# Zero products between periods, smaller GpSimd pieces and 136 score blocks on VectorE in a gated sum of two attentions

## The chip, the cores and the metric

The kernel runs on one core of a Trainium2 chip. A core has TensorE (PE; its weight loads are listed apart as PEld), VectorE (DVE), ScalarE (ACT), GpSimd (POOL), and SyncE (SP), which issues the transfers. The metric is the device time of one execution in microseconds (us); lower is better. A profiled execution also gives the span from the first instruction of the program to the last, the busy time of each engine and TensorE's granted clock.

## The reference, cut to what matters

```python
x = A_x                                            # 1 x 2048 x 512, bf16
g = sigmoid((x * gate_w).sum(-1, keepdims=True))
# A: full attention, 32 heads of 16
p = softmax(einsum("bhqd,bhkd->bhqk", q, k) * 16 ** -0.5)
a = einsum("bhqk,bhkd->bhqd", p, v) -> (S, 512) @ A_wo
# B: each query sees 8 keys, at distances 0, 2, ..., 14
logits = einsum("bhsd,bhswd->bhsw", q, k[pos - 2 * w]) * 16 ** -0.5   # masked below 0
b = einsum("bhsw,bhswd->bhsd", softmax(logits), v[pos - 2 * w]) -> (S, 512) @ B_wo
return g * a + (1 - g) * b
```

## The kernel before

**Attention A.** Queries come in 4 chunks of 512, heads in 8 groups of 4. A *period* is one chunk and one head group; there are 32, ordered so that two chunks alternate over the 8 groups and then the other two. A period has 16 key tiles x 4 heads = 64 score *blocks* of 128 keys x 512 queries. Most blocks go to ScalarE: TensorE writes the scores of a set of three blocks, then of a set of two, into the banks `ring` (`qk`, line 942), ScalarE takes the exponential of the whole set into `pT` (`ex`, 948), and TensorE multiplies with V into the accumulator `acc` (`pv`, 961; `pv_mm`, 909). There is one `acc` bank for all periods. After the last product of a period VectorE copies it out, transposed, into `accT` (`po1`, 1058), and the next period can start to write it; then come a reciprocal (`rden`), a scaling (`ott`) and a second transpose (`oat`).

Some blocks of each period, `n_dve` (line 20), go to VectorE instead: 3 in each of the first 18 periods, then 5, then 6, 129 in all. They come in groups of up to three (`d_group`, 980; groups are made in 1040). TensorE writes each block's scores into a bank `misc` (`dq`), VectorE evicts it into `dt` (`p1`), and three polynomial steps of 128 x (512 times the group's blocks) make the exponential (`p2` and `p3` write `dg`, `p4` writes `pd`); TensorE then adds their product into `acc` as well (`dpv`). There are two `misc` banks. All projections, transposes and the sums of B use them in turn (`misc_ps`).

**Attention B** goes in 16 tiles of 128 queries (`b_tile`, 682). GpSimd multiplies q with eight shifted copies of k, 512 columns an instruction (`prods`, 752), TensorE sums over a head's 16 columns (`sums`), the softmax is on VectorE, ScalarE (one exponential of 128 x 256, `lg`) and GpSimd, and GpSimd multiplies with the shifted v (`avs`, 846) and adds up (`ava`, 860). TensorE transposes the result (`fin`, 880) for the output projection.

**Order.** All instructions of an engine stand in one order that a planner makes before the program is built (`list_schedule`, 98). It holds an estimated duration for each operation (`PE`, `PORT`, `TMUL`, lines 80 to 88) and a due time, and it plays the engines forward, taking the operation that is due first among those that can start. `PORT` is what a VectorE operation takes longer while GpSimd is busy; `TMUL` is the cost of a GpSimd product. Banks and buffers are tokens with a capacity (`Res`, `Tok`).

**Zero products.** The planner also keeps an account of how much TensorE has done over the last 3.4 us (`covered`, 130). Where TensorE would idle over 0.3 us and the account is under 8.6 passes, it books extra products, `o.pre` (line 184). They are products of zeros with ones that are added into the accumulator:

```python
    def zeros(pi, n, first=()):
        js = [j for j in list(first) + list(range(4)) if 1 <= todo[(pi, j)] < NT]
        for k in range(n if js else 0):
            mm(acc_tiles[pi][32 * j:32 * j + 32, :], z32[:], ones_t[:], False, False, tile_position=(0, 32 * j))
```

So they are issued only while a head's accumulation is open; between two periods `js` is empty and nothing is issued, though the account holds them. `warm` (439) issues products of the same kind into a `misc` bank; the old kernel uses it eight times before the first set.

In the profile most lines carry the number of the recording helper (L272 for VectorE, ScalarE, GpSimd and SyncE, L281 for TensorE), so instructions are told apart by their tiles.

Of the kernel before, what the change touches and what calls it, by code (L numbers as in the profile page):

```python
# [9 lines left out]
ALU = mybir.AluOpType  # L10
# [6 lines left out]
CFG = dict(  # L17
    set_sizes=(3, 2),
    chunks_at_once=2,
    n_dve=(3,) * 18 + (5,) * 9 + (6,) * 5,  # L20
    dve_tiles=2,
    b_start=26.0,
    b_space=46.7,
# [3 lines left out]
H = 32  # L27
# [29 lines left out]
class Op:  # L57

    def __init__(self, eng, occ, fn, dl, deps=(), alloc=(), use=(), lat=None, rel=0.0, name="",
                 dense=0, fill=False, after=(), cls="a"):  # L60
        self.sw, self.row = 0.0, False
        if isinstance(occ, str):
            self.row = occ in ("qk", "dq")
            occ, self.sw, lat, dense = PE[occ]
        self.eng, self.occ, self.fn, self.dl, self.rel, self.name = eng, occ, fn, dl, rel, name
        self.dense, self.fill, self.filled = dense, fill, 0
        self.after = [d for d in after if d is not None]
        self.deps, self.alloc = [d for d in deps if d is not None], list(alloc)
        self.lat = (occ if not callable(occ) else occ(False)) + LAT[eng] if lat is None else lat
        self.done = self.ex = None  # L70
        self.cls, self.clock, self.pre = cls, False, 0
        self.slack = SLACK if eng == "pe" else (0.0, 0.0)
        for tk in list(alloc) + list(use):
            tk.ops.append(self)
# [9 lines left out]
          vk=(0.50, 0.05, 0.68, 2), sums=(0.46, 0.15, 0.78, 2), turn=(0.37, 0.02, 0.53, 1), fin=(0.23, 0.10, 0.54, 1),  # L84
          zc=(0.84, 0.10, 0.98, 4), ztr=(0.11, 0.0, 0.24, 0), tr0=(1.0, 0.0, 1.2, 0), tr=(0.55, 0.0, 0.78, 0),
          warm7=(3.2, 0.0, 3.4, 0), warm1=(0.45, 0.0, 0.6, 0))
PORT = dict(p2=0.50, p3=0.75, p4=0.75, ab=0.35, po2=0.48, selk=0.25)
TMUL = 1.35
SLACK, DSLACK = (0.2, 0.2), 2.0
AHEAD = dict(pe=0.10, dve=0.12, act=0.25, pool=0.5, sp=0.0)  # L90


# [2 lines left out]
    return lambda busy: us + (PORT[key] if busy else 0.0)  # L95


def list_schedule(ops):

    INF = 1e18  # L100
    free = {e: 0.0 for e in LAT}
# [24 lines left out]

    out, cover = [], []
    psw = 0.0

    def covered(t):  # L130
        return sum(w * (min(b, t) - max(a, t - SPAN)) for a, b, w in cover if b > t - SPAN and a < t) / PASS
# [10 lines left out]
    def due(o):  # L142
        return o.dl + lag[o.cls]

    def window():
# [8 lines left out]
        end = p.t + p.occ if p.done is not None else max(free["act"], getattr(p, "ready", 0.0)) + p.occ  # L154
        return t, max(t, end - QK_LEAD)

    while len(out) < len(ops):
        best = None
        for e, cs in cand.items():
            if not cs:  # L160
                continue
            es = [(max(free[e], avail(o)), o) for o in cs]
            w = window() if e == "pe" else None
            if w:
                es = [(max(t, w[0]) if o.ex is None and t + o.occ + max(o.sw, 0.0) > w[1] and t < due(o) + LATE else t, o) for t, o in es]
            t0 = min(x[0] for x in es)
            if t0 < INF and (best is None or t0 < best[0]):
                best = (t0, e, es)
# [11 lines left out]
        if e == "pe":  # L180
            idle = t - free[e]
            act = covered(t)
            if t > 30.0 and idle > GAP_MIN and act < ACTIVE:
                o.pre = min(int((idle - 0.05) / FILL), int(ACTIVE - act + 1))
                add_cover(free[e], free[e] + o.pre * FILL, 1.0)
                act = covered(t)
            n = o.dense
            if o.fill and act + n < ACTIVE:
                for k in (2, 1):
                    more = k * FILL  # L190
                    if act + n + k - 1 < ACTIVE and (w is None or t + occ + o.sw + more <= w[1] or act + n + k - 1 < ACTIVE_LOW):
                        o.filled = k
                        occ, lat, n = occ + more, lat + more, n + k
                        break
            add_cover(t, t + (PASS * n if not o.row else PASS), 0.75 if o.row else 1.0)
            psw = o.sw
        o.t, o.done = t, t + max(occ, lat)
        free[e] = t + occ
        if o.ex is not None:
            nq += 1  # L200
        if o.clock:
            lag[o.cls] = t - o.clock
        cand[e].remove(o)
# [10 lines left out]
def kernel(  # L214
# [457 lines left out]
    def opb(*a, **k):  # L672
        return op(*a, cls="b", **k)
# [8 lines left out]
    def b_tile(t):  # L682
# [69 lines left out]
        def prods(hf, w0, w1):  # L752
            def s():
                if w0 == 0:
                    st["prod", hf] = work.tile([128, WH, DC, 128], FP32, name="prod", tag="prod", bufs=2)
                for w_ in range(w0, w1):
                    b0 = PAD - DIL * (hf * WH + w_)
                    G.tensor_tensor(out=st["prod", hf][:, w_], in0=kT_tiles[t][:, :, b0:b0 + 128], in1=st["qT"][:], op=ALU.mult)
            return s

        def sums(hf, w0, w1):
# [84 lines left out]
        def avs(hf, w0, w1):  # L846
            def s():
                if hf + w0 == 0:
                    st["ob"] = work.tile([128, D], FP32, name="ob", tag="ob", bufs=1)
                if w0 == 0:  # L850
                    st["av", hf] = work.tile([128, WH, D], FP32, name="prod", tag="prod", bufs=2)
                vsh, attn, pr_ = st["vsh"], st["lg"], st["av", hf]
                for w_ in range(w0, w1):
                    a0 = attn[:, :, hf * WH + w_:hf * WH + w_ + 1]
                    G.tensor_tensor(out=pr_[:, w_, :].rearrange("p (h d) -> p h d", d=DH),
                                    in0=vsh[:, hf * WH + w_, :].rearrange("p (h d) -> p h d", d=DH),
                                    in1=_ap(a0, [list(a0.ap[0]), [W, H], [0, DH]]), op=ALU.mult)
            return s

        def ava(hf):  # L860
            def s():
                pr_ = st["av", hf]
                for w_ in range(2):
                    G.tensor_tensor(out=pr_[:, w_, :], in0=pr_[:, w_, :], in1=pr_[:, 2 + w_, :], op=ALU.add)
                G.tensor_tensor(out=(pr_[:, 0, :] if hf else st["ob"][:]), in0=pr_[:, 0, :], in1=pr_[:, 1, :], op=ALU.add)
                if hf:
                    st["obb"] = work.tile([128, D], BF16, name="obb", tag="obb", bufs=1)
                    G.tensor_tensor(out=st["obb"][:], in0=st["ob"][:], in1=pr_[:, 0, :], op=ALU.add)
            return s
        for hf in range(2):  # L870
            tpv = tok("prod", 2)
            for w0 in (0, 2):
                a = opb("pool", 2 * TMUL - 0.2, avs(hf, w0, w0 + 2), tb + 22 + 10 * hf + 1.5 * w0, deps=[a, lv],
                        alloc=([tpv] if w0 == 0 else []) + ([tob] if hf + w0 == 0 else []), use=[tlg, tvs] + ([tpv] if w0 else []))
            a = opb("pool", 4.9 + 1.6 * hf, ava(hf), tb + 28 + 10 * hf, deps=[a], alloc=[tbb] if hf else [], use=[tpv, tob])
        tk = tok("misc", 2)
        if cb not in obt_tok:
            obt_tok[cb] = tok("obt", 2)
# [11 lines left out]
        def oe():  # L890
            V.tensor_copy(out=obt_tiles[cb][:, :, tl * 128:(tl + 1) * 128], in_=st["ptp"][:])
        a = opb("pe", "fin", fin, tb + 50, deps=[a] + o_obt[-1:], alloc=[tk] + ([obt_tok[cb]] if tl == 0 else []), use=[tbb] + ([obt_tok[cb]] if tl else []))
        o_obt.append(opb("dve", 0.34, oe, tb + 51, deps=[a], use=[tk, obt_tok[cb]]))

    for t in range(NT):
# [36 lines left out]
    for k, us in enumerate(sets):  # L932
# [25 lines left out]
        for pi in pis:  # L958
            mine = [(s_, t, j) for s_, (p_, t, j) in enumerate(us) if p_ == pi]

            def pv(pi=pi, mine=mine, st=st):
                zeros(pi, st["op", pi].filled, [j for _, t, j in mine])
                for s_, t, j in mine:
# [2 lines left out]
            o = op("pe", "pv", pv, tn - 2.0, fill=not first, deps=[b] + [o_v[(4 * periods[pi][1] + j, t)] for _, t, j in mine]  # L966
                   + ([] if first else [o_first[pi]]),
                   alloc=[acc_tok[pi]] if first else [], use=[tp] + ([] if first else [acc_tok[pi]]), name=f"pv{k}")
            o.slack = (0.0, 0.0)
            st["op", pi] = o  # L970
            if first:
                o_first[pi] = o
# [2 lines left out]
                t_first[pi] += sum(1 for _, t, j in mine if t == 0)  # L975
                o_t0[pi] = o

    d_last = [None, None]

    def d_group(pi, gr, lo, hi):  # L980
        c_, i = periods[pi]
# [38 lines left out]
                pv_mm(pi, t, j, st["pd"][:, q_, :], vd_all[:, t - (NT - NTD)])  # L1020

        dur = 0.14 + 0.54 * n
        prev2, prev = d_last
        for q_, (t, j) in enumerate(gr):
            tx = tok("misc", 2)
            a = op("pe", "dq", dq(q_), hi - 7.5 + q_, deps=[o_q[pi], o_kc[i][t // TPC], prev2] + ([o_k0[t // TPC]] if i == 0 else []), alloc=[tx], use=[q_tok[pi]],
                   rel=lo, name=f"dq{pi}")
            prev2, prev = prev, op("dve", 0.67, p1(q_), hi - 6.5 + q_, deps=[a], alloc=[td] if q_ == 0 else [],
                                   use=[tx] + ([td] if q_ else []), after=[prev])
        d_last[:] = prev2, prev  # L1030
        a = op("dve", shared(dur, "p2"), p2, hi - 4.2, deps=[prev], alloc=[tg], use=[td])
        a = op("dve", shared(dur, "p3"), p3, hi - 2.6, deps=[a], use=[tg, td])
        a = op("dve", shared(dur, "p4"), p4, hi - 1.0, deps=[a], alloc=[tp], use=[tg, td])
        a = op("pe", "dpv", pv, hi, deps=[a, o_t0[pi]] + [o_v[(4 * i + j, t)] for t, j in gr],
               use=[tp, acc_tok[pi]], name=f"dpv{pi}")
        a.slack = (DSLACK, 0.0)
        o_pv[pi].append(a)

    for pi in range(NP):
# [143 lines left out]
        b = op("dve", 0.67, t_ev, E2 + 1 + tt, deps=[b, a], alloc=[tos], use=[tk, tfb])  # L1183
        op("sp", 0.6, dout, E2 + 2 + tt, deps=[b], use=[tos], lat=2.2)

    order = list_schedule(ops)
    if cfg.get("debug"):
        cfg["debug"](order)
    for o in order:
        if o.pre and acc_tiles:  # L1190
            zeros(max(acc_tiles), o.pre)
        o.fn()


# [28 lines left out]
```

## Time and profile before

| | us |
|---|---|
| median of 3 runs (lowest to highest) | 923.12 (919.32 to 923.97) |
| the profiled execution | 919.24 |
| its span | 917.5 |
| ScalarE busy | 885.3 |
| TensorE busy | 828.3 |
| VectorE busy | 647.1 |
| GpSimd busy | 554.3 |

The page gives each engine's busy time and its share of the span. In a group of instructions the columns are: output and inputs, shape, count, busy time in us, mean ns of one, and the idle time of the engine just before them with what ended most of it. In a timeline the columns are start, length in us, engine and operation; instructions that follow each other closely are merged into one row (x44 is 44 of them, and the shape shown is that of the first), and the idle time before a row stands in brackets with what ended it. The table by stretches gives, for each, the busy time and count of each engine, the granted clock, and the share and rate of transfers. A granted clock of 1.00 is full speed; a clock of 0.73 over 25 us is the mean of full and half speed.

### The profile page before, as it was taken

Reading aid. Unit: us, or ns where it says so; the run is one execution under the profiler, and the core shown is the slowest. Engines: PE = TensorE matmul, PEld = TensorE weight load, DVE = VectorE, ACT = ScalarE, POOL = GpSimd, SP = SyncE. Lnnn points to the kernel's source line nnn. Section 1 sums busy time; section 2 is a strip of 40 time slices with the busy share of each in tenths; the row PEclk is TensorE's granted clock in tenths of the full one; section 3 lists DMA queues with packets and bytes.
Section 4 is the critical chain, followed back from the end, with each engine's and each line's share of the span. In section 5 each row is a group of like instructions: output and inputs, shape, how many; then the busy total and the mean of one; then the engine's idle time right before and its main releaser. Section 6 shows DMA issues by size and latency. Waiting matters only on the chain.

```text
span 917.5 us, 20157 instructions
## 1 busy us (share of the span) xinstructions
PE 828.3 (90%) x8520; PEld 306.6 (33%) x8520; DVE 647.1 (71%) x815; ACT 885.3 (96%) x794; POOL 554.3 (60%) x412
## 2 busy tenths in 40 slices
PE   7999989999999999998999999989898889899886
PEld 4333333333433333333333232333332333222222
DVE  4596676776567765676934677787868686978874
ACT  4999999999999999999999999999999999989996
POOL 1347492687567696677574839985979883910000
PEclk9999999999999999999999998999998999979999
DMA  8101010010101010101010100110010110000001
GB/s 272 57 4 51 2 43 12 7 47 7 47 8 53 1 48 7 47 7 53 1 64 30 53 8 1 52 47 8 1 53 2 47 52 2 1 1 1 1 1 46
DMA packets 27330, 28.58 MB, mean 31 GB/s; under 512 B 1604, under 2 KB 26724, under 8 KB 27240
## 3 DMA queue, kind: packets, MB, share of 16 engines
q1 hardware_dynamic: 27240, 27.30, 9.2%
q8 instruction: 66, 1.08, 0.5%
q14 instruction: 24, 0.20, 0.1%
HBM read 23.08 MB, written 4.22 MB: 30 GB/s over the span
## 4 chain that ended last, share of the span: by engine, by line
ACT 56%; issue 20%; PE 18%; DVE 5%; DMA 1%; SPq 0%; DVEq 0%; ACTq 0%
ACT pT L272 55%; PE acc L281 6%; PE ring L281 6%; PE misc_ps L281 4%; DVE dg L272 2%; PE misc L281 1%; DVE pd L272 1%; DMA xld<-in_A_x_dram 1%; ACT lg L272 1%; DVE dt L272 0%; DVE osb L272 0%; ACT xT L272 0%; DVE accT L272 0%; DVE qt L272 0%; DVE kmax_all L272 0%
## 5 line engine op out<-in xcount | busy, mean ns | idle before, releaser
L272 ACT ACTIVATE pT<-ring 128x1536 bf16<-128x1536 f32 (+2 forms) x768 | 874.7, 1353 | 12.1 <-PE ring L281 11.3
L281 PE MATMUL ring<-qt,kt_all 32*128 32x512 bf16 x1919 | 311.0, 387 | 71.1 <-ACT pT L272 66.3
L281 PE MATMUL acc<-pT,vp_all 128*17 128x512 bf16 (+1 forms) x1919 | 298.6, 390 | 1.1 <-DVE accT L272 0.9
L272 POOL TENSOR_TENSOR prod<-kTb,qTb 128x512 f32<-128x512 bf16 x128 | 167.8, 1334 | 99.1 <-DVE qTb L272 87.0
L281 PEld LDWEIGHTS <-kt_all 32*128 32x128 bf16 x2048 | 109.6, 91 | 342.7 <-issue 329.5
L272 POOL TENSOR_TENSOR prod<-vsh,lg 128x512 f32<-128x512 bf16 x128 | 181.4, 1441 | 3.1 <-PE misc_ps L281 1.9
L272 POOL TENSOR_TENSOR prod<-prod 128x512 f32<-128x512 f32 x80 | 130.3, 1645 | 1.3
L272 DVE TENSOR_SCALAR dt<-misc 128x512 f32<-128x512 f32 x129 | 87.1, 683 | 58.6 <-PE misc L281 53.4
L281 PEld LDWEIGHTS <-vp_all 128*17 128x17 bf16 (+1 forms) x1919 | 68.6, 88 | 160.9 <-issue 156.9
L281 PE MATMUL misc_ps<-xT,wst 128*32 128x512 bf16 x1024 | 100.2, 383 | 1.1 <-ACT kt_all L272 0.8
L281 PE MATMUL acc<-ones_t,z 128*32 128x512 bf16 x271 | 94.7, 397 | 0.0
L272 DVE SCALAR_TENSOR_TENSOR pd<-dg,dt 128x1536 uint16<-128x1536 bf16 (+1 forms) x46 | 94.1, 2046 | 0.3
L272 DVE SCALAR_TENSOR_TENSOR dg<-dt,dg 128x1536 bf16<-128x1536 uint16 (+1 forms) x46 | 93.0, 2022 | 0.4
L272 DVE SCALAR_TENSOR_TENSOR dg<-dt 128x1536 bf16<-128x1536 uint16 (+1 forms) x46 | 90.5, 1966 | 1.2
L272 POOL TENSOR_TENSOR lg<-lg,rr 128x256 f32<-128x256 f32 x16 | 10.1, 628 | 134.3 <-DVE rr L272 47.5
L281 PE MATMUL misc<-qt,kt_all 32*128 32x512 bf16 x129 | 47.9, 390 | 2.7 <-DVE qt L272 1.6
L281 PE MATMUL misc_ps<-prod,hsel 128*32 128x128 f32 x1024 | 43.0, 276 | 1.5 <-DVE dt L272 0.8
L272 DVE TENSOR_SCALAR qt<-misc_ps,rowc 128x512 bf16<-128x512 f32 x32 | 25.7, 803 | 20.4 <-PE misc_ps L281 20.3
L281 PE MATMUL misc_ps<-xT,bw 128*128 128x128 bf16 x512 | 39.2, 220 | 0.0
L272 DVE TENSOR_TENSOR qt<-qt,misc_ps 128x512 bf16<-128x512 bf16 x32 | 21.7, 678 | 17.6 <-PE misc_ps L281 17.6
L281 PEld LDWEIGHTS <-bw 128*128 128x128 bf16 x512 | 28.7, 98 | 15.9 <-issue 15.4
L281 PEld LDWEIGHTS <-wst 128*32 128x32 bf16 x1024 | 27.8, 95 | 18.6 <-issue 5.5
(85 smaller groups left out, 620.6 us busy)
## 6 DMA issues: line engine op xcount, KB each, us to landing
vsh<-v_scr SPq DMA_DIRECT2D x16, 1024.0 KB, 5.5
xld<-in_A_x_dram SPq DMA_DIRECT2D x4, 512.0 KB, 7.4
v_scr<-vs SPq DMA_DIRECT2D x16, 128.0 KB, 1.7
out_dram<-osb SPq DMA_DIRECT2D x16, 128.0 KB, 1.7
wst<-in_A_wqkv_dram SPq DMA_DIRECT2D x3, 512.0 KB, 7.0
bw<-in_B_wqkv_dram SPq DMA_DIRECT2D x1, 1536.0 KB
bwo<-in_B_wo_dram SPq DMA_DIRECT2D x1, 512.0 KB, 13.4
woarr<-in_A_wo_dram SPq DMA_DIRECT2D x8, 64.0 KB, 10.0
```

The costliest lines, as they stand in the source:

```text
L272: return chain_on(key, f(*a, **k))
L281: return chain(nc.tensor.matmul(out, lhsT=lhsT, rhs=rhs, start=start, stop=stop, **kw))
```

## The change

- `n_dve`: periods 1 to 14 take 3 and 4 blocks in turn; 136 blocks in all, and ScalarE has 1912 instead of 1919. Four blocks make two groups of two.
- GpSimd's products and sums are issued in pieces of 256 columns, so 368 more instructions.
- Planner costs: `PORT` is lowered, `TMUL` and the cost of the sums are raised.
- Planner rules: near the end of a period (at most two of its products into `acc` left) a long polynomial step (`long`) that would run into the copy of `acc` is planned behind it (`turn`). The score products of a VectorE group do not start before the last polynomial step of the group ahead (`behind`). The transposes of a B tile are planned 4 us after GpSimd's end.
- Zero products are booked for `acc` only while a period's accumulation is partly done; between periods they go into a free `misc` bank (`pre_misc`, through `warm`), if there is time after the bank's last reader, and they take the bank's turn.

```diff
-    n_dve=(3,) * 18 + (5,) * 9 + (6,) * 5,
+    n_dve=(3, 4) * 7 + (3,) * 4 + (5,) * 9 + (6,) * 5,
...
-PORT = dict(p2=0.50, p3=0.75, p4=0.75, ab=0.35, po2=0.48, selk=0.25)
-TMUL = 1.35
-SLACK, DSLACK = (0.2, 0.2), 2.0
+PORT = dict(p2=0.30, p3=0.42, p4=0.42, ab=0.20, po2=0.28, selk=0.15)
+TMUL = 1.58
+SLACK, DSLACK, TURN = (0.2, 0.2), 2.0, 0.5
...
+    def turn():
+
+        p = min((p for p in acc_all if acc_left[p] > 0), default=None)
+        if p is None or acc_left[p] > 2:
+            return None
+        rest = [o for o in acc_ops[p] if o.done is None]
+        if any(d.done is None for o in rest for d in o.deps):
+            return None
+        return max(max(d.done + o.slack[0] for d in o.deps) for o in rest) + TURN
...
+            if e == "dve":
+                tt = turn()
+                if tt is not None:
+                    es = [(max(t, tt) if o.long and t + o.occ(False) > tt and t < tt else t, o) for t, o in es]
...
-                o.pre = min(int((idle - 0.05) / FILL), int(ACTIVE - act + 1))
-                add_cover(free[e], free[e] + o.pre * FILL, 1.0)
+                k = min(int((idle - 0.05) / FILL), int(ACTIVE - act + 1))
+                if any(0 < acc_left[p] < acc_all[p] for p in acc_all):
+                    o.pre = k
+                    add_cover(free[e], free[e] + k * FILL, 1.0)
+                elif not any(tk.res is misc for tk in o.alloc):
+                    n = len(misc.order)
+                    us = [u.done for u in misc.order[n - misc.cap].ops] if n >= misc.cap else [0.0]
+                    if None not in us:
+                        b = max([free[e]] + us)
+                        k = min(k, int((t - b - 0.05) / FILL))
+                        if k > 0:
+                            o.pre_misc = k
+                            add_cover(b, b + k * FILL, 1.0)
...
-                    G.tensor_tensor(out=st["prod", hf][:, w_], in0=kT_tiles[t][:, :, b0:b0 + 128], in1=st["qT"][:], op=ALU.mult)
+                    for c in range(0, DC, 2):
+                        G.tensor_tensor(out=st["prod", hf][:, w_, c:c + 2], in0=kT_tiles[t][:, c:c + 2, b0:b0 + 128],
+                                        in1=st["qT"][:, c:c + 2], op=ALU.mult)
...
+                for d0 in range(0, D, D // 2):
+                    ds = slice(d0, d0 + D // 2)
+                    for w_ in range(2):
+                        G.tensor_tensor(out=pr_[:, w_, ds], in0=pr_[:, w_, ds], in1=pr_[:, 2 + w_, ds], op=ALU.add)
...
+        a.slack = (4.0, 0.2)
...
-        prev2, prev = d_last
+        prev2, prev, behind = d_last
...
-                   rel=lo, name=f"dq{pi}")
+                   rel=lo, after=[behind], name=f"dq{pi}")
...
         a = op("dve", shared(dur, "p2"), p2, hi - 4.2, deps=[prev], alloc=[tg], use=[td])
+        a.long = True
...
+        if o.pre_misc:
+            warm(o.pre_misc)()
         o.fn()
```

More of the change, by code (lines that the diff above doesn't have):

```diff
@@ L70, in __init__ @@
         self.done = self.ex = None
-        self.cls, self.clock, self.pre = cls, False, 0
+        self.cls, self.clock, self.pre, self.pre_misc, self.acc, self.long = cls, False, 0, 0, None, False
         self.slack = SLACK if eng == "pe" else (0.0, 0.0)
@@ L95, in shared, with list_schedule @@
     return lambda busy: us + (PORT[key] if busy else 0.0)
-def list_schedule(ops):
+def list_schedule(ops, misc):
     INF = 1e18
@@ L128, in list_schedule @@
     psw = 0.0
+    acc_left, acc_all, acc_ops = {}, {}, {}
+    for o in ops:
+        if o.acc is not None:
+            acc_all[o.acc] = acc_left[o.acc] = acc_all.get(o.acc, 0) + 1
+            acc_ops.setdefault(o.acc, []).append(o)
     def covered(t):
@@ L183, in list_schedule @@
             if t > 30.0 and idle > GAP_MIN and act < ACTIVE:
-                o.pre = min(int((idle - 0.05) / FILL), int(ACTIVE - act + 1))
-                add_cover(free[e], free[e] + o.pre * FILL, 1.0)
+                k = min(int((idle - 0.05) / FILL), int(ACTIVE - act + 1))
[11 more added lines that the diff above has]
+                            add_cover(b, b + k * FILL, 1.0)
+                            f = Op("pe", 0.0, None, 0.0)
+                            f.done = b + k * FILL + 0.25
+                            tk = Tok(misc)
+                            tk.ops.append(f)
+                            misc.order.append(tk)
                 act = covered(t)
@@ L200, in list_schedule @@
             nq += 1
+        if o.acc is not None:
+            acc_left[o.acc] -= 1
         if o.clock:
@@ L853, in s @@
                 for w_ in range(w0, w1):
[L854 to L857, printed above, removed]
+                    for h0 in range(0, H, H // 2):
+                        a0 = attn[:, h0:h0 + H // 2, hf * WH + w_:hf * WH + w_ + 1]
+                        ds = slice(h0 * DH, (h0 + H // 2) * DH)
+                        G.tensor_tensor(out=pr_[:, w_, ds].rearrange("p (h d) -> p h d", d=DH),
+                                        in0=vsh[:, hf * WH + w_, ds].rearrange("p (h d) -> p h d", d=DH),
+                                        in1=_ap(a0, [list(a0.ap[0]), [W, H // 2], [0, DH]]), op=ALU.mult)
             return s
@@ L862, in s @@
                 pr_ = st["av", hf]
-                for w_ in range(2):
-                    G.tensor_tensor(out=pr_[:, w_, :], in0=pr_[:, w_, :], in1=pr_[:, 2 + w_, :], op=ALU.add)
-                G.tensor_tensor(out=(pr_[:, 0, :] if hf else st["ob"][:]), in0=pr_[:, 0, :], in1=pr_[:, 1, :], op=ALU.add)
                 if hf:
                     st["obb"] = work.tile([128, D], BF16, name="obb", tag="obb", bufs=1)
-                    G.tensor_tensor(out=st["obb"][:], in0=st["ob"][:], in1=pr_[:, 0, :], op=ALU.add)
+                for d0 in range(0, D, D // 2):
+                    ds = slice(d0, d0 + D // 2)
+                    for w_ in range(2):
+                        G.tensor_tensor(out=pr_[:, w_, ds], in0=pr_[:, w_, ds], in1=pr_[:, 2 + w_, ds], op=ALU.add)
+                    G.tensor_tensor(out=(pr_[:, 0, ds] if hf else st["ob"][:, ds]), in0=pr_[:, 0, ds], in1=pr_[:, 1, ds], op=ALU.add)
+                    if hf:
+                        G.tensor_tensor(out=st["obb"][:, ds], in0=st["ob"][:, ds], in1=pr_[:, 0, ds], op=ALU.add)
             return s
@@ L872, in b_tile @@
             for w0 in (0, 2):
-                a = opb("pool", 2 * TMUL - 0.2, avs(hf, w0, w0 + 2), tb + 22 + 10 * hf + 1.5 * w0, deps=[a, lv],
+                a = opb("pool", 2 * TMUL, avs(hf, w0, w0 + 2), tb + 22 + 10 * hf + 1.5 * w0, deps=[a, lv],
                         alloc=([tpv] if w0 == 0 else []) + ([tob] if hf + w0 == 0 else []), use=[tlg, tvs] + ([tpv] if w0 else []))
-            a = opb("pool", 4.9 + 1.6 * hf, ava(hf), tb + 28 + 10 * hf, deps=[a], alloc=[tbb] if hf else [], use=[tpv, tob])
+            a = opb("pool", 5.7 + 2.3 * hf, ava(hf), tb + 28 + 10 * hf, deps=[a], alloc=[tbb] if hf else [], use=[tpv, tob])
         tk = tok("misc", 2)
@@ L968 @@
                    alloc=[acc_tok[pi]] if first else [], use=[tp] + ([] if first else [acc_tok[pi]]), name=f"pv{k}")
-            o.slack = (0.0, 0.0)
+            o.slack, o.acc = (0.0, 0.0), pi
             st["op", pi] = o
@@ L976 @@
                 o_t0[pi] = o
-    d_last = [None, None]
+    d_last = [None, None, None]
     def d_group(pi, gr, lo, hi):
@@ L1026, in d_group @@
             a = op("pe", "dq", dq(q_), hi - 7.5 + q_, deps=[o_q[pi], o_kc[i][t // TPC], prev2] + ([o_k0[t // TPC]] if i == 0 else []), alloc=[tx], use=[q_tok[pi]],
-                   rel=lo, name=f"dq{pi}")
+                   rel=lo, after=[behind], name=f"dq{pi}")
             prev2, prev = prev, op("dve", 0.67, p1(q_), hi - 6.5 + q_, deps=[a], alloc=[td] if q_ == 0 else [],
                                    use=[tx] + ([td] if q_ else []), after=[prev])
-        d_last[:] = prev2, prev
         a = op("dve", shared(dur, "p2"), p2, hi - 4.2, deps=[prev], alloc=[tg], use=[td])
+        a.long = True
         a = op("dve", shared(dur, "p3"), p3, hi - 2.6, deps=[a], use=[tg, td])
+        a.long = True
         a = op("dve", shared(dur, "p4"), p4, hi - 1.0, deps=[a], alloc=[tp], use=[tg, td])
+        a.long = True
+        d_last[:] = prev2, prev, a
         a = op("pe", "dpv", pv, hi, deps=[a, o_t0[pi]] + [o_v[(4 * i + j, t)] for t, j in gr],
                use=[tp, acc_tok[pi]], name=f"dpv{pi}")
-        a.slack = (DSLACK, 0.0)
+        a.slack, a.acc = (DSLACK, 0.0), pi
         o_pv[pi].append(a)
@@ L1184 @@
         op("sp", 0.6, dout, E2 + 2 + tt, deps=[b], use=[tos], lat=2.2)
-    order = list_schedule(ops)
+    order = list_schedule(ops, res["misc"])
     if cfg.get("debug"):
```

## The prediction

> **What bounds the kernel now.** I read the page's busy shares and the slices first, then ScalarE's timeline, then the stretches with their granted clock.
>
> ```profile
> PE 828.3 (90%) x8520; PEld 306.6 (33%) x8520; DVE 647.1 (71%) x815; ACT 885.3 (96%) x794; POOL 554.3 (60%) x412
> PEclk9999999999999999999999998999998999979999
> ```
>
> ScalarE is busy 96% and its only large work is the 767 exponentials of the score sets. The clock row shows that TensorE's granted clock fell in a few slices. What ScalarE lost is not its idle time (12.1 us in its group): successive exponentials overlap by 0.1 to 0.4 us, so a late set first eats the overlap. I therefore measure pace, start to start, on its timeline.
>
> ```profile
> 255.89 49.82 ACT L272 ACTIVATE pT<-ring 128x1536 bf16<-128x1536 f32 x44
> 305.51 0.51 ACT L272 ACTIVATE lg<-lg 128x256 f32<-128x256 f32 x1
> ...
> 799.20 9.25 ACT L272 ACTIVATE pT<-ring 128x1536 bf16<-128x1536 f32 x8 [0.51 <-PE ring L281]
> 809.36 2.37 ACT L272 ACTIVATE pT<-ring 128x1536 bf16<-128x1536 f32 x2 [0.91 <-PE ring L281]
> 812.37 2.36 ACT L272 ACTIVATE pT<-ring 128x1536 bf16<-128x1536 f32 x2 [0.64 <-PE ring L281]
> 815.37 1.45 ACT L272 ACTIVATE pT<-ring 128x1536 bf16<-128x1536 f32 x1 [0.64 <-PE ring L281]
> 817.28 91.17 ACT L272 ACTIVATE pT<-ring 128x1024 bf16<-128x1024 f32 x81 [0.46 <-PE ring L281]
> ```
>
> Sets alternate between three blocks and two, so 44 sets are 110 blocks, and from 255.89 to 305.51 they took 49.62 us: 0.4511 us a block with nothing in the way. The exponentials run from 21.23 to 908.45 (817.28 + 91.17), 887.2 us. At that pace 1919 blocks are 865.7; the 16 softmax exponentials of B, one slot of 0.30 us each (305.51 to the next start at 305.81), are 4.8. **Lost: 16.7 us.** Where: from 799.20 to 817.28 there are 13 sets, 33 blocks, 14.9 us at pace, but 18.1 passed: 3.2 lost. The same sum over the other stretches whose granted clock is below 1.00 gives 1.2 (305.81 to 337.68), 2.05 (539.64 to 562.89), 0.8 (634.95 to 668.23) and 2.07 (683.33 to 699.84). Together 9.3 us go with five falls of the clock; 7.4 are spread elsewhere, largest 1.25 near 757.
>
> ```profile
> 795.00:820.00 25.00, 22.48 (x136) 5.01 (x135) 19.24 (x19) 21.77 (x20) 11.18 (x6) 0.73 0.01 1
> 820.00:908.50 88.50, 78.63 (x720) 25.07 (x720) 61.04 (x68) 88.45 (x79) 0.00 (x0) 1.00 0.01 4
> ```
>
> The columns are TensorE, weight load, VectorE, ScalarE, GpSimd, granted clock. A fall begins at the end of a period. This is the one at 802:
>
> ```profile
> 800.71 1.76 DVE L272 SCALAR_TENSOR_TENSOR dg<-dt 128x1536 bf16<-128x1536 uint16 x1
> ...
> 802.39 0.71 DVE L272 STREAM_TRANSPOSE accT<-acc 128x512 f32<-128x512 f32 x1
> 802.96 0.39 PE L281 MATMUL ring<-qt,kt_all 32*128 32x512 bf16 x3 [0.95 <-ACT pT L272]
> ```
>
> A long polynomial step holds VectorE, the copy of acc waits behind it, and TensorE, which has no accumulator to write, stands idle 0.95 us; matmuls take 0.61 us in place of 0.39 from 804.20 on.
>
> **The change, part by part.** *136 blocks on VectorE.* Seven blocks leave ScalarE: 7 x 0.4511 = **-3.2 us** on the path. On VectorE they are 14 groups of two in place of 7 of three, and seven more evictions of 0.683.
>
> ```profile
> L272 DVE SCALAR_TENSOR_TENSOR dg<-dt 128x1536 bf16<-128x1536 uint16 x37 | 76.9, 2079 | 1.1
> ...
> L272 DVE SCALAR_TENSOR_TENSOR dg<-dt 128x1536 bf16<-128x1536 uint16 x6 | 10.5, 1758 | 0.2
> ```
>
> The first row is the whole run, the second the stretch 826 to 908, where GpSimd has ended. A three-step polynomial of three blocks costs 2079 + 2112 + 2108 = 6.30 us beside GpSimd and 1758 + 1732 + 1738 = 5.23 without. For two blocks the run has 1505 + 1650 + 1790 = 4.95, or by proportion 3.49 alone. So VectorE gets 14 x 3.49 - 7 x 5.23 + 4.8 = +17 at the least and 14 x 4.95 - 7 x 6.30 + 4.8 = +30 at the most. It hides under VectorE's 270 us idle; without that cover it would come back as late products of VectorE's blocks at a period's end.
>
> *GpSimd in pieces of 256.* The order of the built program has 368 more GpSimd instructions.
>
> ```profile
> 788.30 1.27 POOL L272 TENSOR_TENSOR ob<-prod 128x512 f32<-128x512 f32 x1
> ...
> L272 POOL TENSOR_TENSOR lg<-lg,rr 128x256 f32<-128x256 f32 x16 | 10.1, 628 | 134.3 <-DVE rr L272 47.5 <-ACT pT L272 37.7 <-PE misc L281 16.1
> ```
>
> An undisturbed 512-column step takes 1.27 and a 256-column one 0.628, so two pieces cost 1.26: nothing. The upper bound, a fixed 0.1 us for each added piece, is 37 us over the 16 tiles of B. GpSimd's last instruction ends at 806.33 (803.67 + 2.66), and in the changed order its last tile is folded in after block 1775 of 1912 instead of 1733 of 1919, some 20 us later; the end of the run is 100 us away, which covers even the bound. What it brings: a long VectorE step that meets GpSimd waits for the instruction in flight. The excess is 1.07 a group of three (37 groups: 39.6), 1.46 a group of two (nine: 13.1), and 0.37 at each ott step (786 in the run, 413 alone; 32: 11.9): 64.6 us, of which half goes if the instruction in flight is half as long, 32. That pays for the added blocks, and the steps in front of the copy of acc get shorter. For GpSimd I take no gain: a product stands at 2.62 (789.52) instead of 1.09 when VectorE's step came first, and the steps are as long as before.
>
> *Copies kept free, later scores.* Long polynomial steps are held back when the copy of acc is due. VectorE then idles up to one step (1.76) a period, 56 us in 32 periods at the most, within its 270; behind the held step stand the rest of its group and then that group's product into acc, for which only the next copy waits, most of a period (27 us) later. The late copy at 802 cost 0.95 us of TensorE. Score products for VectorE stand behind the preceding group's last step in the plan, so they no longer hold a misc bank early; what they delay is VectorE's eviction (dt), which already waits 53.4 us for them in VectorE's own idle time. The first transposes of a finished B tile are planned 4 us after GpSimd instead of 0.2; they are needed only by the output projections of their chunk, a wait that costs nothing until then. The smaller port costs and larger GpSimd cost only shift the plan.
>
> *Zero products between periods.* Today's plan books products between periods that are never issued (with no open accumulator the list is empty) and counts them as cover. The changed program issues 26 into a misc bank, at 14 places, all but one after block 1510; products into acc go from 271 to 257. A zero product takes 0.397 as a row and 0.21 in step; it fills an idle TensorE, so it costs nothing while its bank is free.
>
> *Sum.* Of the 9.3 lost with the clock, 3.2 lie in the late third where the new products are; the other four places (6.1) get none and profit only from the quicker copy and from a plan that no longer counts absent work: I take 0.6 of it, 3.7, so 6.9 in all, with bounds 0 and 9.3. Of the 7.4 spread losses I take 0.65, 4.8, since the largest two I could follow (1.25 near 757, 0.65 before 799.20) stand behind VectorE: the chain of waits runs through dg, dg and pd from 747.69 to 755, and at 798.08 TensorE waits 0.89 for qt; bounds -2 (new waits) and 7.4. The head (21.23) and tail (9.05) stay. 919.24 (the profiled execution: span 917.5 and 1.7 around it) - 3.2 - 6.9 - 4.8 = **904 us**. The runs' median, 923.12, is 3.9 above that execution; I put it down to more falls of the clock in those runs, which the change would thin too, and keep 904.
>
> **The rivals.** *The clock falls as often.* For: four of five places get no product, and five falls at 31 boundaries leave much to chance. Against: the phantom cover is gone everywhere. Time: 919.2 - 3.2 - 2.4 (half of my spread gain) = 913.6. "TensorE: Matmul & The Clock Gate", section Part 1, in the Trainium skill gives this rival its mechanism: activity is judged in free-running windows of 3.4 us, so the phase of a run decides. The granted stretches here (0.73 of 25 us is 13.6 us at half clock, four such windows) agree.
>
> *It does not do what it says.* The plan's new costs may fit the chip no better, and waits only move: the seven blocks alone give 916.0.
>
> *Slower: the zero products block TensorE.* They stand in order before the next scores and need a bank that VectorE has read. Behind a polynomial step (2.1) with one set in ScalarE's hand (0.9) each place loses 1.2; at all 14 places 16.8, so 919.2 - 3.2 + 16.8 = 932.8. It decides from eight places on (9.6 us, which beats 3.2 and the 4.6 of the bound below). Against: the plan puts them only where the bank is free with time over, and the waits of TensorE's misc products for VectorE and ScalarE sum to 10.4 us in the whole run, none over 1.5.
>
> **How the numbers follow.** A measurement of this kernel tells 0.5%, 4.6 us, from no change. Forecast 0.68, clock falls on 0.16, blocks alone 0.08, blocked TensorE 0.08. Faster: all of the first, 0.10 of the second, 0.01 of the third: 0.79; same 0.13; slower 0.08. Range: the low end is 919.2 - 3.2 - 9.3 - 7.4 = 899.3, less 3 for a pace between the 0.4511 used and the fastest pairs; the high end takes in the clock rival and stops short of the third: 896 to 915.
>
> **What would show it.** Right: ScalarE at 0.451 a block from first to last set, at most two stretches with a clock below 1.00, long steps near 1.9 rather than 2.08, GpSimd's pieces near 0.55 to 0.63 where nothing blocks them. Wrong: half-clock stretches at the same four boundaries, ScalarE waiting for ring right behind zero products, or GpSimd running past 880 and the last projections behind it.

## The result, and the profile after

The changed kernel takes 906.72 us (median of 4 runs, 904.43 to 907.0); the kernel before 921.39 (4 runs, 919.32 to 923.97). The ratio is 0.986, with a 95% interval of 0.982 to 0.990, so faster by 1.4%; the medians lie 14.7 us apart. The profiled execution took 906.7, its span is 904.6 (before: 919.24 and 917.5). Of the runs further down, one execution of e8 took 3622.6 us and is left out of every number.

From the page, busy times and granted clock:

```profile
PE 822.2 (91%) x8532; PEld 308.6 (34%) x8532; DVE 638.5 (71%) x843; ACT 879.4 (97%) x791; POOL 637.1 (70%) x780
PEclk9999999999999999999999999999999999999999
```

No slice shows a granted clock below nine tenths any more. VectorE has 53 groups of polynomial steps instead of 46 and is busy 9 us less; GpSimd is busy 83 us more.

ScalarE's timeline, a clean stretch and the places where a set came late:

```profile
340.74 54.37 ACT L309 ACTIVATE pT<-ring 128x1024 bf16<-128x1024 f32 x48
394.79 0.61 ACT L309 ACTIVATE lg<-lg 128x256 f32<-128x256 f32 x1
...
551.66 18.33 ACT L309 ACTIVATE pT<-ring 128x1536 bf16<-128x1536 f32 x16
570.48 12.75 ACT L309 ACTIVATE pT<-ring 128x1536 bf16<-128x1536 f32 x11 [0.48 <-PE ring L318]
...
772.14 32.82 ACT L309 ACTIVATE pT<-ring 128x1024 bf16<-128x1024 f32 x29
805.29 54.49 ACT L309 ACTIVATE pT<-ring 128x1536 bf16<-128x1536 f32 x48 [0.34 <-PE ring L318]
860.25 34.99 ACT L309 ACTIVATE pT<-ring 128x1536 bf16<-128x1536 f32 x31 [0.46 <-PE ring L318]
```

The pace is unchanged: 48 sets, 120 blocks, in 54.05 us from 340.74 to 394.79, 0.4504 a block. The exponentials run from 21.54 to 895.24 (860.25 + 34.99), 873.7 us. At 0.4511 the 1912 blocks are 862.5 and B's exponentials 4.8, so 6.4 us are lost, where 16.7 were before. The stretches with a lowered clock:

```profile
551.66:583.00 31.34, 29.04 (x290) 10.81 (x290) 25.45 (x31) 30.86 (x29) 30.71 (x36) 0.95 0.02 6
772.14:805.29 33.15, 29.32 (x229) 9.55 (x228) 26.89 (x30) 32.82 (x30) 32.60 (x34) 0.96 0.02 8
805.29:895.24 89.95, 81.00 (x727) 25.31 (x724) 56.23 (x60) 89.47 (x79) 4.47 (x3) 0.98 0.01 4
```

Against the pace they lost 0.67 (68 blocks), 0.67 (72) and 1.09 (197): 2.4 us, where five stretches lost 9.3 before. Narrower stretches show each of the three falls:

```profile
564.00:574.00 10.00, 9.49 (x68) 2.33 (x66) 8.43 (x7) 9.52 (x9) 10.00 (x10) 0.83 0.04 13
799.00:809.00 10.00, 9.02 (x57) 2.26 (x52) 8.03 (x6) 9.66 (x10) 9.69 (x10) 0.83 0.01 2
854.00:864.00 10.00, 8.87 (x55) 2.46 (x55) 8.06 (x7) 9.54 (x10) 0.00 (x0) 0.83 0.00 0
```

10 us at 0.83 are 3.4 us at half clock; the fall before at 802 lasted 13.6. They also stand elsewhere. In the kernel before, each of the five falls begins 1.0 to 3.1 us behind a copy of `acc` (copies at 330.8, 554.3, 663.2, 691.3 and 802.4, falls at 334, 556, 665, 692 and 805). In the changed kernel they begin in the middle of a period, at 567, 803 and 857, 11 us or more behind the last copy. So in this execution the falls at the ends of periods are gone, and the three that are left stand in mid-period.

VectorE's steps and GpSimd's pieces, mean ns behind the busy time:

```profile
L309 POOL TENSOR_TENSOR prod<-kTb,qTb 128x256 f32<-128x256 bf16 x256 | 209.5, 849 | 106.9 <-DVE qTb L309 89.7 <-PE misc_ps L318 16.8
...
L309 DVE SCALAR_TENSOR_TENSOR dg<-dt 128x1536 bf16<-128x1536 uint16 x30 | 58.6, 1952 | 1.0
...
L309 DVE SCALAR_TENSOR_TENSOR dg<-dt 128x1024 bf16<-128x1024 uint16 x23 | 31.1, 1351 | 0.7
```

A three-block step costs 1952 ns instead of 2079 (1758 without GpSimd), so VectorE waits less for GpSimd. A pair of pieces costs GpSimd 2 x 849 = 1.70 us in place of 1.334: undisturbed, one takes 0.607 at the least, and a whole one took 1.039, and each piece may have to wait for a VectorE step (not followed one by one). GpSimd ends at 809.9 all the same (806.3 before).

### The profile page after: what moved, and what is told of

The parts are those of the page before. It is cut to its first block, busy times and chain, and to the rows that moved or that the text cites. A ratio compares the mean times of both kernels' runs of the same rounds, so it can differ in the third digit from the quotient of the medians.

```text
span 904.6 us, 20592 instructions
## 1 busy us (share of the span) xinstructions
PE 822.2 (91%) x8532; PEld 308.6 (34%) x8532; DVE 638.5 (71%) x843; ACT 879.4 (97%) x791; POOL 637.1 (70%) x780
## 4 chain that ended last, share of the span: by engine, by line
ACT 62%; issue 21%; PE 15%; DVE 1%; DMA 1%; ACTq 0%; SPq 0%; DVEq 0%
ACT pT L309 61%; PE ring L318 5%; PE acc L318 5%; PE misc_ps L318 4%; ACT lg L309 1%; DMA xld<-in_A_x_dram 1%; PE misc L318 1%; ACT xT L309 0%; DVE osb L309 0%; DVE kmax_all L309 0%; PE pxt L495 0%; PE misc_ps L820 0%; PE misc_ps L930 0%; ACT kt_all L309 0%; ACTq L1268 0%
## 5 line engine op out<-in xcount | busy, mean ns | idle before, releaser
L309 ACT ACTIVATE pT<-ring 128x1536 bf16<-128x1536 f32 x765 | 870.1, 1387 | 4.5 <-PE ring L318 4.3
L318 PE MATMUL ring<-qt,kt_all 32*128 32x512 bf16 x1912 | 302.5, 383 | 69.5 <-ACT pT L309 63.9
L318 PE MATMUL acc<-pT,vp_all 128*17 128x512 bf16 (+1 forms) x1912 | 289.0, 385 | 1.1 <-DVE accT L309 0.9
L309 POOL TENSOR_TENSOR prod<-kTb,qTb 128x256 f32<-128x256 bf16 x256 | 209.5, 849 | 106.9 <-DVE qTb L309 89.7
L318 PEld LDWEIGHTS <-kt_all 32*128 32x128 bf16 x2048 | 112.4, 91 | 339.2 <-issue 325.6
L309 POOL TENSOR_TENSOR prod<-vsh,lg 128x256 f32<-128x256 bf16 x256 | 207.0, 840 | 7.7 <-PE misc_ps L318 7.0
L309 POOL TENSOR_TENSOR prod<-prod 128x256 f32<-128x256 f32 x160 | 140.4, 893 | 2.5
L309 DVE TENSOR_SCALAR dt<-misc 128x512 f32<-128x512 f32 x136 | 91.7, 686 | 68.7 <-PE misc L318 65.7
L318 PE MATMUL misc_ps<-xT,wst 128*32 128x512 bf16 x1024 | 97.5, 384 | 0.8 <-ACT kt_all L309 0.8
L318 PE MATMUL acc<-ones_t,z 128*32 128x512 bf16 x257 | 89.2, 388 | 0.0
L309 DVE TENSOR_SCALAR qt<-misc_ps,rowc 128x512 bf16<-128x512 f32 x32 | 25.5, 798 | 14.1 <-PE misc_ps L318 14.0
L318 PEld LDWEIGHTS <-bw 128*128 128x128 bf16 x512 | 28.7, 98 | 14.7 <-issue 14.4
```

The costliest lines, as they stand in the source:

```text
L309: return chain_on(key, f(*a, **k))
L318: return chain(nc.tensor.matmul(out, lhsT=lhsT, rhs=rhs, start=start, stop=stop, **kw))
```

## The experiments

Each ratio is to the runs of the kernel before that stood beside it. *Half clock* is the mean over the runs of 2 x (1 - granted clock) x span, the time for which TensorE had half its clock, head and tail of the run included. *Without it* is the mean time with 0.273 us taken off for each us of half clock; that slope comes from the 57 runs of the kernel before, whose half clock went from 20 to 55 us and whose times from 914.6 to 924.6 (correlation 0.94).

| run | median us | ratio (95%) | half clock us | without it us |
|---|---|---|---|---|
| before (57 runs beside the experiments) | 919.2 | | 35 | 909.7 |
| changed | 906.7 | 0.986 (0.982 to 0.990) | 13 | 902.6 |
| e1_nozero | 914.6 | 0.995 (0.993 to 0.997) | 47 | 902.5 |
| e2_whole | 911.7 | 0.992 (0.990 to 0.995) | 23 | 906.7 |
| e3_pieces | 922.5 | 1.004 (1.002 to 1.007) | 39 | 912.4 |
| e4_136 | 914.1 | 0.994 (0.992 to 0.996) | 9 | 912.1 |
| e5_noturn | 907.8 | 0.987 (0.983 to 0.990) | 12 | 904.4 |
| e6_nobehind | 914.6 | 0.996 (0.993 to 0.998) | 20 | 909.7 |
| e7_129 | 912.2 | 0.992 (0.989 to 0.995) | 13 | 908.6 |
| e8_oldcosts | 917.8 | 0.999 (0.996 to 1.001) | 20 | 912.7 |
| e9_tmul154 | 906.6 | 0.985 (0.982 to 0.988) | 8 | 904.7 |
| e10_poolold | 914.9 | 0.994 (0.992 to 0.997) | 21 | 909.4 |
| e11_portold | 912.8 | 0.992 (0.989 to 0.995) | 9 | 910.7 |
| e12_more | 907.6 | 0.985 (0.983 to 0.988) | 9 | 905.0 |

The first three experiments keep a plan as it is and change only what is issued; all others plan anew.

**The zero products alone (e1).**

```diff
-        if o.pre_misc:
-            warm(o.pre_misc)()
```

> The changed kernel in its own order, with the 26 zero products between periods not issued. If these products keep the clock up (my theory gives them about half of the 6.9 us of the clock term), the granted clock falls at one to three of the seven late boundaries where they stood (after block 1510), ScalarE loses 1 to 3.5 us more, and the time is 908 to 910 against 906.7. If the new order alone does it (rival), 906 to 907 and no more falls than the changed kernel's three.

914.6: my theory's direction, but above both ranges; the loss is over twice what I gave the products. ScalarE's timeline of this run, in the stretch where the first falls come:

```profile
717.55 2.55 ACT L309 ACTIVATE pT<-ring 128x1024 bf16<-128x1024 f32 x2 [0.46 <-PE ring L318]
720.56 1.02 ACT L309 ACTIVATE pT<-ring 128x1024 bf16<-128x1024 f32 x1 [0.47 <-PE ring L318]
722.98 4.62 ACT L309 ACTIVATE pT<-ring 128x1536 bf16<-128x1536 f32 x4 [1.39 <-PE ring L318]
```

Its two halves by stretches (granted clock is the third number from the end):

```profile
21.50:700.00 678.50, 628.27 (x6714) 240.73 (x6713) 485.96 (x647) 677.29 (x610) 526.32 (x660) 1.00 0.09 28
700.00:895.00 195.00, 174.40 (x1483) 54.82 (x1482) 135.68 (x148) 188.76 (x167) 101.75 (x108) 0.91 0.04 13
```

All its falls lie after 700, where the products had stood. Three of the four begin 1.2 to 2.8 us behind a copy of `acc` at which there had been products (copies at 711.0, 739.9 and 794.4); the fourth lasts from 871 to 885, over the copy at 875.7, another such place. Time without half clock is that of the changed kernel (902.5 and 902.6): the 26 products cost nothing, and in this order they are worth 34 us of half clock, about 8 us by the medians (9 by the slope).

Up to 700 the clock holds in this one execution, while the kernel before fell at 334, 556, 665 and 692. That the new order is enough there is not shown: in the same order the changed kernel fell at 567, and e2, which follows, at 296 and 569.

**GpSimd's pieces alone (e2, e3).** e2 is the changed kernel with 512-column instructions, e3 the kernel before with 256-column ones; the products, for example:

```diff
 # e3 (e2 is the reverse, in the changed kernel)
-                    G.tensor_tensor(out=st["prod", hf][:, w_], in0=kT_tiles[t][:, :, b0:b0 + 128], in1=st["qT"][:], op=ALU.mult)
+                    for c in range(0, DC, 2):
+                        G.tensor_tensor(out=st["prod", hf][:, w_, c:c + 2], in0=kT_tiles[t][:, c:c + 2, b0:b0 + 128],
+                                        in1=st["qT"][:, c:c + 2], op=ALU.mult)
```

> The changed kernel in its own order, with GpSimd's instructions whole again (512 columns). If the shorter wait for GpSimd's instruction in flight pays (my theory: 32 us of VectorE time, which the order now counts on), the long VectorE steps return to about 2.08 us, copies of acc and score evictions come late against the plan, and the time is 911 to 917. If the order alone does it, 906 to 908; if whole pieces help because GpSimd is 14% faster with them, below 906.

> The kernel before in its own order, with only GpSimd's instructions cut into pieces of 256 columns. If the pieces pay by themselves, the time is 914 to 918 (of the spread loss of 7.4 us a half goes, and the clock falls less often); if only together with an order made for them, 919 to 923; if GpSimd's extra 26 us of its own work hurts, above 923.

e2 is 5 us slower than the changed kernel, as expected, and its steps are longer again, 2045 ns where the changed kernel has 1952:

```profile
L309 DVE SCALAR_TENSOR_TENSOR dg<-dt 128x1536 bf16<-128x1536 uint16 x30 | 61.4, 2045 | 1.0
```

As only the pieces differ, this is their worth in the new order. e3 is slower than the kernel before by 0.4%, as expected if pieces pay only with an order made for them. The waits of its TensorE, from the table of who waited for whom (us, times, longest), show a new wait; in the kernel before no matmul waited for GpSimd:

```profile
ACT pT L272 <- PE ring L281: 14.6, 16, 3.8
...
PE misc_ps L893 <- POOL obb L272: 5.2, 3, 2.7
```

GpSimd is slower in pieces, the old order has the transposes of its result (`fin`) where whole instructions would have been done, and the next score sets stand behind them: matmuls wait at 624.4 and 683.3, and right after, at 625.3 and 685.2, ScalarE's sets come late by 1.6 and 4.2 us against the pace (the second during a fall of the clock, from 682 to 688). So pieces by themselves do not pay, and the new order needs them.

**136 blocks in the old plan (e4).** `n_dve` of the changed kernel in the kernel before.

> The kernel before with 136 blocks on VectorE and a new plan under the old costs and rules. My theory: seven blocks are 3.2 us of ScalarE and nothing else, 917 to 919 against 921.4. Rival: the 17 to 30 us more of VectorE work without shorter waits come back as late copies, 920 to 925.

914.1, better than either expected, because the clock falls less: half clock is 9 us instead of 35. Neither theory had that, and it is luck in the sense that this plan was not made for it. Without it the time is 912.1, not below the 909.7 of before. In its profiled execution the exponentials run from 21.39 to 902.80; at the same pace 14.1 us are lost, with one fall of 3.4 us inside, where the kernel before lost 7.4 outside its five. So the seven blocks' 3.2 us are given back in waits, as the rival said (its three-block steps take 1.96 to 2.14 us).

This plan has no zero products between periods and the old account of them. So a plan can hold the clock without either, and the drop of half clock from 35 to 13 us is no proof that the new rules made it; e1 shows only what the products do in the order that has them.

**The plan's rules (e5, e6).**

```diff
 # e5
-            if e == "dve":
+            if False:
                 tt = turn()
 # e6
-                   rel=lo, after=[behind], name=f"dq{pi}")
+                   rel=lo, name=f"dq{pi}")
```

> The changed kernel, newly planned without the rule that holds long VectorE steps back before the copy of acc; its order has 24 zero products in misc banks instead of 26. The times of all runs so far lie on a line in the half-clock time (before: 910 us plus 0.26 per us of half clock; changed: 903 plus 0.23). If the rule is what lowered the intercept, the intercept goes back up by 2 to 5 us and the time is 910 to 914; if it is of no weight, 906 to 909.

> The changed kernel, newly planned without the later scores; only 5 zero products then find a free misc bank, in place of 26. If the later scores matter by freeing the banks for zero products, half-clock time returns to 35 to 50 us and the time is 911 to 915, as without the products. If the scores' own lateness is what helps, the intercept rises as well, 915 or more. If neither, 906 to 908.

Without the held-back steps the time is 907.8, within the interval of the changed kernel: no weight that could be told. Without the later scores it is 914.6. Half clock rises little (20 us, not the 35 to 50 that the lost zero products were to bring; 297 go into `acc` instead of 257, which may be why); it is the time without it that rises, by 7. So the later scores seem to help by themselves, in this one plan. ScalarE's two largest waits in this run stand at falls of the clock, at 771 and 798; the next is outside them, at 505.77. They make up only a part of the 7 us, and the rest was not followed:

```profile
505.77 2.37 ACT L309 ACTIVATE pT<-ring 128x1536 bf16<-128x1536 f32 x2 [0.93 <-PE acc L318]
...
774.36 4.73 ACT L309 ACTIVATE pT<-ring 128x1536 bf16<-128x1536 f32 x4 [1.16 <-PE ring L318]
...
800.79 100.46 ACT L309 ACTIVATE pT<-ring 128x1536 bf16<-128x1536 f32 x89 [1.07 <-PE ring L318]
```

**129 blocks in the new plan (e7).** `n_dve` of before in the changed kernel.

> The changed kernel, newly planned with the 129 blocks of before; 18 zero products in misc banks. My theory: seven blocks more on ScalarE, 3.2 us, so 910. If the 136 blocks cost VectorE what they save ScalarE, 907.

912.2, above both expected times, and 5.4 us above the changed kernel by the two ratios, where the blocks explain 3.2; the other 2 may belong to this plan.

**The plan's costs (e8, e10, e11), and a plan's luck (e9).**

```diff
 # e8: both; e10: the GpSimd costs alone; e11: the port costs alone; e9: TMUL = 1.54
 # e8 and e10 also take back the planned durations of the products with v and of the sums (not shown)
-PORT = dict(p2=0.30, p3=0.42, p4=0.42, ab=0.20, po2=0.28, selk=0.15)
-TMUL = 1.58
+PORT = dict(p2=0.50, p3=0.75, p4=0.75, ab=0.35, po2=0.48, selk=0.25)
+TMUL = 1.35
```

> The changed kernel, newly planned with the old port costs and GpSimd costs; 20 zero products in misc banks. If the plan's costs only shift the order (my prediction gave them nothing), 906 to 909. If costs that fit the pieces are what makes VectorE's steps come when TensorE needs them, the part of ScalarE's loss outside half-clock stretches rises from 11.8 to 15 or more and the time is 910 to 914.

> The changed kernel planned with a GpSimd cost of 1.54 in place of 1.58, a change too small to mean anything: it shows what a new plan alone can do to the time. If single plans are a fair test of a rule, 905 to 909; if a plan's luck is as large as the effects found so far, anything from 903 to 914, and the verdicts on single rules (later scores, blocks) must be widened by that.

> The changed kernel planned with the old GpSimd costs alone (port costs as changed). If the plan puts TensorE's sums before GpSimd's products are ready when it takes GpSimd for too fast, TensorE waits for GpSimd's products (3.4 us in 8 waits with all old costs) and the time is 914 to 919, as with all old costs. If the port costs did it, 906 to 909.

> The changed kernel planned with the old port costs alone (GpSimd costs as changed). The counterpart: 906 to 909 if GpSimd's costs are what matters, 912 to 918 if the port costs are.

e9 hardly differs from the changed kernel (906.6), and so does e12 further down: neighbouring plans lie within 2.5 us without half clock, so the 7 to 10 us of e6, e8, e10 and e11 are hardly a plan's luck alone, though each is a single plan. All three neighbours (e5, e9, e12) lie 2 us above the changed kernel in that column (904.4 to 905.0 against 902.6), so some 2 us of its lead may be luck. With all old costs the gain is gone: 917.8, beyond both ranges that I had given. Both halves matter: the old GpSimd costs alone leave 914.9, the old port costs alone 912.8, so my expectation of e11 for the case that GpSimd's are what matters (906 to 909) missed. The waits of e8, and the one line that answers to it in the changed kernel:

```profile
ACT pT L309 <- PE ring L318: 12.2, 13, 3.8
...
PE misc_ps L318 <- POOL prod L309: 3.4, 8, 1.7
```

```profile
ACT pT L309 <- PE ring L318: 4.3, 8, 2.1
```

The largest of these waits, and the set behind it, in e8:

```profile
662.26 0.41 PE L318 MATMUL misc_ps<-prod,hsel 128*32 128x128 f32 x4 [1.66 <-POOL prod L309]
...
665.71 1.45 ACT L309 ACTIVATE pT<-ring 128x1536 bf16<-128x1536 f32 x1 [3.78 <-PE ring L318]
```

A plan that takes GpSimd for faster than it is puts TensorE's sums before their products are ready; TensorE waits in order, and the scores behind it come late. (The clock falls there too, from 664 on, so not all of the 3.78 us is GpSimd's.) e10 has such waits as well (2.3 us in five). In the changed kernel no matmul waits for GpSimd's products. That explains only a part: in e11 no matmul waits for GpSimd either, and its time without half clock is 8 us above the changed kernel's. How the port costs act is not shown. Shorter steps alone are not the gain: with both old costs, in e8, they take 1886 ns, less than the changed kernel's 1952.

**A try for more (e12).** `ACTIVE` 9.2 instead of 8.6, so more zero products are booked.

> A try for a faster version: the changed kernel planned with a higher target for TensorE's activity (ACTIVE 9.2 in place of 8.6), so that more zero products are booked. The changed kernel still spends some 13 us at half clock, at 0.23 to 0.29 us each: if more products take most of it away, 903 to 905; if they only make the score sets later, 907 to 910.

907.6, ratio 0.985, in the range for products that make the sets later: not to be told from the changed kernel. Half clock falls to 9 us, but the time without it is 2 us higher. No version tried beats the changed kernel by more than its interval.

## Why the prediction was right, point by point

- **The time**: 904 forecast, 906.7 measured, inside 896 to 915. From the profiled execution 15.2 us were to go, 12.5 went; by the medians 14.7. The size is right partly by luck: as the points below show, the way in which it came about is not that of the sum.
- **Seven blocks, -3.2**: the pace stayed, so 3.2 is what they take off ScalarE. In the one old-rule plan that was tried (e4) they are worth nothing; e7 agrees with them in the new one (5.4, with 2 unexplained). The sets of before are 768, not 767; no sum uses that.
- **The clock, -6.9**: 9.3 lost before, 2.4 after, 6.9. The size is right; its split was not. I let the products hold one place of 3.2 us and the four others profit by six tenths. e1 shows the products to be worth about 8 us by themselves: without them half clock is 47 us, more than the 35 of before, so the new order and account alone, which had more than half of the term, do not lower it. The quicker copy that was part of their reason shows no gain either (e5). Of the signs named, none of the four boundaries without products has a fall again, but three stretches are below 1.00 where at most two were to be.
- **Spread losses, -4.8**: 7.4 before, 4.0 after (6.4 less 2.4), 3.4. Over the runs the same stands in the time without half clock: 909.7 to 902.6 is 7.1, of which 3.2 are the blocks and 3.9 the rest. So the term was over by one us. The mechanism was half right: shorter waits for GpSimd are there (1952 ns instead of 2079) and are needed (e2), but by themselves they lose time (e3).
- **Head and tail** were to stay; the first exponential starts 0.3 later and the tail is 0.3 longer.
- **VectorE's account**: 17 to 30 us more for the blocks and 32 less for the pieces; it is busy 9 less, in between.
- **GpSimd in pieces, "nothing", at most 37 us**: wrong. GpSimd is busy 83 us more. The 0.628 us of the `lg` step was not the price of a 256-column product (0.607 to 0.73 undisturbed, against half of 1.039 to 1.27), and twice as many instructions met VectorE's steps. It stayed without effect on the end because GpSimd still finished 95 us before it, as reasoned (3.6 us later than before, where I had some 20).
- **"The smaller port costs and larger GpSimd cost only shift the plan"**: wrong, the largest miss of the working. The gain hangs on that shift: with the old costs the time is 917.8.
- **Transposes 4 us later, "a wait that costs nothing"**: not tried alone. e3, without it, has 5.2 us of TensorE in three waits for those results, and the changed kernel has none; that the 4 us are the reason is not shown.
- **Later scores, no term of their own**: 7 us in e6. I had them as freeing banks; e6 issues 5 products between periods instead of 26, but its loss is not in half clock.
- **Held-back steps**: they cost nothing, as reasoned, but nothing is shown to come from them either (e5).
- **The rivals.** Half clock went from 35 to 13 us in the mean, so the clock does not fall as often. The change does more than the blocks: ScalarE lost 6.4 us instead of 16.7. TensorE is not blocked by the zero products (e1: the same time without half clock with them and without). The guess that the median of before stood above its profiled execution through more falls of the clock fits the line through 57 runs; no granted clock was kept for those first runs.

What stays open: how much of e6, e8, e10 and e11 belongs to the rule or cost and how much to the one plan that was drawn, how the port costs act, the 2 us of e7, and whether another plan under the old rules would have held the clock as e4 does. e11, too, has only 9 us of half clock, with 8 products between periods.

## What to carry to other kernels

Where one engine is busy 96%, measure its pace start to start in a clean stretch and sum what each stretch lost: the share of busy time hid 16.7 us here, and the ledger by stretches gave each term of the forecast. A planner's estimated durations are part of the kernel: cutting GpSimd's work into pieces made it busy 15% longer (a pair of products 27%), and it paid only in an order made with durations that fit. Filler for TensorE is best counted only where it is issued, though no run tried the account alone; in this order 26 products at the ends of periods were worth 8 us and cost nothing. Judge a plan by several neighbouring ones: they differed by 2 us here.

## What the runs showed of the hardware

- The time of this kernel follows the half-clock time of TensorE run by run: 0.27 us for each us, over 57 runs of one and the same program, from 914.6 to 924.6. The correlation of 0.94 leaves about a ninth of its scatter (its variance) to anything else.
- A GpSimd product of 256 columns takes 0.607 us at the least where one of 512 takes 1.039, so a pair costs 17% more undisturbed; in the run a pair cost 1.70 against 1.334.
- In the traces of all 14 kernels a stretch of half clock between the first and the last exponential lasts 3.4 us or two, three or four times that (3.4 each in the changed kernel, 13.6 at 802 in the kernel before).
